# 384 unused bytes ahead of the x tiles: the moving operands shifted to the weights' address modulo 512

## The chip, the cores and the metric

The kernel runs on one core of a Trainium2 chip. The metric is device time in microseconds (us) of one execution. The runs before took 1220.17, 1220.52 and 1220.63 us; the median is 1220.52 us.

## What is computed

The reference is a causal convolution over seven steps with softmax weights per head, then a gated layer (SwiGLU, 192 to 1536 and back), then an ELU layer (192 to 2048 and back), all in float32:

```python
w = softmax(weight)                                   # (8 heads, 7 taps)
x = einsum('hk,bskhg->bshg', w, windows(x, 7))        # x: (2, 4096, 192) -> 8192 tokens of 192
g = x @ w_gate                                        # (192, 1536)
x = (g / (1 + exp(-g)) * (x @ w_val)) @ w_out         # (1536, 192)
h = x @ w_in                                          # (192, 2048)
out = where(h > 0, h, exp(min(h, 0)) - 1) @ w_out2    # (2048, 192)
```

## The kernel before

Tokens go through in 16 blocks of 512 (`TB`). Each block has a first layer (12 units j of 128 columns of both gate and value) and a second layer (16 units, taken two at a time). Stages of the two layers alternate over the blocks; the first two blocks are mixed while the weights still come in.

Every product is made in reduced-precision passes: an operand is split into a rounded part (`hi`) and the rest (`lo`), and hi·hi, lo·hi and hi·lo are summed in PSUM. The weights come as 64-bit words and are split once, into `in1hi`, `in1lo`, `in2hi`, `in2lo` (lines 386 and 387) and `out1`, `out2` (line 437), which stay in SBUF to the end. The activations are split block by block: x (the convolved input) and y (between the layers) into tiles of the pool `xp` (line 503), h (a layer's inner activations) into tiles of the pool `hp` (line 712).

On TensorE each matmul takes 64 rows (one half of the partitions, `lower` or `upper`), a stationary weight slice of 64x128 and a moving slice of 64x512. Two matmuls, one for each half of the rows, are always issued one after the other (lines 414 to 420 for the way into a layer, lines 467 and 468 for the way out), and the array runs both halves side by side. In this text a *step* is such a pair: one matmul of the lower half and one of the upper. Into a layer a unit takes nine steps, out of it five. For each matmul a weight load (LDWEIGHTS) of 128 columns goes ahead.

The order on all engines is written by a planner (class `Plan`) from fixed costs; it knows nothing of addresses. Tiles get their SBUF addresses from pools, which are laid one behind the other in the order in which they are made (lines 180 to 191). So a tile's address follows from the sizes of what was made before it.

One place in this kernel already has activations among the weights. While block 1's first layer runs, the second layer's weight tiles are still empty, and the h of its units j = 0 to 8 are written into them: even j into `in2hi` and `in2lo`, odd j into `out2` (lines 919 to 931, used by `split`, line 708). In the trace the matmuls that stream these read `c<-in2hi,out`, `c<-in2lo,out` and `c<-out,out`, where all others of the way out read `c<-h,out`. The first name after the arrow is the moving operand, the second the weights; buffer numbers are left out, so `out` stands for `out1` and `out2`.

Of the kernel before, what the change touches and what calls it, by code (L numbers as in the profile page):

```python
# [7 lines left out]
F32 = mybir.dt.float32  # L8
# [8 lines left out]
P = 128  # L17
# [147 lines left out]
def tile_conv_swiglu_elu(ctx: ExitStack, tc: tile.TileContext, x, weight, words, out, FF1, FF2):  # L165
# [16 lines left out]
    xs_p = ctx.enter_context(tc.tile_pool(name="xs", bufs=2))  # L182
    cv_p = ctx.enter_context(tc.tile_pool(name="cv", bufs=2))
    x_p = ctx.enter_context(tc.tile_pool(name="xp", bufs=1))
    y_p = ctx.enter_context(tc.tile_pool(name="yp", bufs=1))
    h_p = ctx.enter_context(tc.tile_pool(name="hp", bufs=7))
    t_p = ctx.enter_context(tc.tile_pool(name="tp", bufs=4))
# [882 lines left out]
```

## Time and profile before

| what | value |
|---|---|
| runs, median (lowest to highest) | 1220.52 us (1220.17 to 1220.63) |
| profiled execution, span from first to last instruction | 1218.3 us |
| median less span (what lies around the instructions) | 2.2 us |
| TensorE matmul (PE) busy | 1208.2 us, 99% |
| VectorE (DVE) busy | 990.4 us, 81% |
| ScalarE (ACT) busy | 837.2 us, 69% |
| DMA | 31.86 MB moved, mean 26 GB/s |

The page gives the profiled execution by its span alone. PE busy is the union of the matmuls' records; a matmul of 64x512 is recorded at about 391 ns although one starts about every 117 ns, so the records overlap and a busy PE says nothing of its pace. The pace is read from start to start.

### The profile page before, as it was taken

The numbers are of one execution on the slowest core, as the hardware profiler recorded it, in microseconds if no ns is written. First come the engines' busy times: TensorE is split into PE (matmuls) and PEld (weight loads), VectorE is DVE, ScalarE is ACT, GpSimd is POOL, SyncE is SP. The second block draws the span as 40 slices with busy tenths as digits, with TensorE's granted clock in tenths as the row PEclk, the third lists the DMA queues.
The fourth block names the chain that finished last, engine by engine and source line by source line (L and its number), as shares of the span: only waits on it lengthen the run. The fifth ranks groups of instructions, "written<-read, shape, count | busy, mean of one in ns | idle before, by whom it ended". The sixth has DMA issues, their size and how long they took to land.

```text
span 1218.3 us, 25292 instructions
## 1 busy us (share of the span) xinstructions
PE 1208.2 (99%) x10285; PEld 1143.1 (94%) x10285; DVE 990.4 (81%) x1632; ACT 837.2 (69%) x1556; POOL 2.1 (0%) x15
## 2 busy tenths in 40 slices
PE   8999999999999999999999999999999999999998
PEld 6899998999989999999999999999999999999987
DVE  8999999798695977959779596895968868495697
ACT  8878787585774857758477584866748667485686
POOL 0000000000000000000000000000000000000000
PEclk9999999999999999999999999999999999999999
DMA  5424000101000010000100001010000000000000
GB/s 187 143 64 142 14 19 6 49 1 36 1 23 15 1 36 1 23 14 1 36 1 23 14 3 34 1 34 4 10 14 1 23 1 11 13 1 15 2 14 14
DMA packets 18597, 31.86 MB, mean 26 GB/s; under 512 B 2864, under 2 KB 9008, under 8 KB 18480
## 3 DMA queue, kind: packets, MB, share of 16 engines
q1 hardware_dynamic: 18464, 30.25, 8.4%
q8 instruction: 80, 1.31, 0.5%
q14 instruction: 37, 0.30, 0.1%
q10 hardware_dynamic: 16, 0.00, 0.0%
HBM read 19.75 MB, written 6.29 MB: 21 GB/s over the span
## 4 chain that ended last, share of the span: by engine, by line
PE 98%; DVE 1%; ACT 0%; DMA 0%; issue 0%; DVEq 0%
PE c L468 43%; PE ph L416 22%; PE pv L416 18%; PE pg L416 15%; DVE cv L639 0%; DMA x<-x 0%; DMA wraw<-in_weight_dram 0%; ACT L222 0%; DVE w L323 0%; ACT words L338 0%; ACT x L538 0%; DVE p L845 0%; DVE o L890 0%; ACT o L886 0%; ACT cv L636 0%
## 5 line engine op out<-in xcount | busy, mean ns | idle before, releaser
L468 PE MATMUL c<-h,out 64*128 64x512 f32 x4390 | 707.9, 391 | 0.0
L468 PEld LDWEIGHTS c<-h,out 64*128 64x128 f32 x4390 | 554.3, 184 | 29.9
L416 PE MATMUL pv<-x,in1hi 64*128 64x512 f32 x1152 | 417.8, 393 | 0.0
L416 PE MATMUL pg<-x,in1hi 64*128 64x512 f32 x1152 | 411.1, 393 | 1.8 <-DMA x<-x 1.8
L716 ACT CAST h<-t 128x512 fp32r<-128x512 f32 x439 | 274.2, 625 | 176.3 <-DVE t L747 113.0
L720 DVE TENSOR_TENSOR h<-t,h 128x512 fp32r<-128x512 f32 x439 | 301.2, 687 | 80.5 <-ACT h L716 75.2
L416 PE MATMUL ph<-y,in2hi 64*128 64x512 f32 x1536 | 350.2, 392 | 0.0
L416 PEld LDWEIGHTS ph<-y,in2hi 64*128 64x128 f32 x1536 | 239.1, 184 | 8.0 <-DVE t L789 0.4
L416 PE MATMUL pg<-x,in1lo 64*128 64x512 f32 x576 | 225.6, 392 | 0.0
L416 PE MATMUL pv<-x,in1lo 64*128 64x512 f32 x576 | 225.6, 392 | 0.0
L416 PE MATMUL ph<-y,in2lo 64*128 64x512 f32 x768 | 222.1, 392 | 0.0
L416 PEld LDWEIGHTS pv<-x,in1hi 64*128 64x128 f32 x1152 | 212.2, 185 | 7.0 <-ACT x L538 0.3
L416 PEld LDWEIGHTS pg<-x,in1hi 64*128 64x128 f32 x1152 | 210.0, 185 | 9.1 <-ACT w L315 2.2
L747 DVE TENSOR_TENSOR t<-t,pv 128x512 f32<-128x512 f32 x192 | 131.4, 684 | 103.5 <-ACT t L743 79.8
L743 ACT ACTIVATE t<-pg 128x512 f32<-128x512 f32 x192 | 114.3, 595 | 139.6 <-PE pg L416 137.7
L785 DVE SCALAR_TENSOR_TENSOR t<-t,th 128x512 f32<-128x512 f32 x256 | 174.7, 686 | 25.5 <-ACT t L781 23.8
L789 DVE SCALAR_TENSOR_TENSOR t<-ph,t 128x512 f32<-128x512 f32 x256 | 172.6, 686 | 4.3
L777 ACT ACTIVATE th<-ph 128x512 f32<-128x512 f32 x256 | 153.2, 598 | 20.0 <-PE ph L416 18.2
L781 ACT ACTIVATE t<-ph 128x512 f32<-128x512 f32 x256 | 154.1, 602 | 0.0
L416 PEld LDWEIGHTS ph<-y,in2lo 64*128 64x128 f32 x768 | 129.4, 184 | 3.8
L639 DVE SCALAR_TENSOR_TENSOR cv<-xs,taps,cv 128x512 f32<-128x512 f32 (+1 forms) x180 | 109.6, 621 | 1.6
L416 PEld LDWEIGHTS pv<-x,in1lo 64*128 64x128 f32 x576 | 106.4, 185 | 3.0 <-DVE in1lo L350 0.2
(71 smaller groups left out, 566.8 us busy)
## 6 DMA issues: line engine op xcount, KB each, us to landing
words<-in_words_dram SPq DMA_DIRECT2D x34, 384.0 KB, 3.3
x<-x SPq DMA_DIRECT2D x64, 64.0 KB, 1.9
out_dram<-o SPq DMA_DIRECT2D x16, 256.0 KB, 2.0
xs<-in_x_dram SPq DMA_DIRECT2D x14, 259.0 KB, 3.0
out_dram<-o SPq DMA_DIRECT2D x16, 128.0 KB, 2.3
xs<-in_x_dram SPq DMA_DIRECT2D x30, 65.5 KB, 2.7
xs<-in_x_dram SPq DMA_DIRECT2D x2, 256.0 KB, 3.1
xs<-in_x_dram SPq DMA_DIRECT2D x2, 64.0 KB, 3.5
```

What stands on the lines that cost most here:

```text
L416: nc.tensor.matmul(p[bank][:, :n], w[r, k, g], m[r, s, :n], start=i == 0, stop=i == len(seq) - 1)
L468: nc.tensor.matmul(p[:, :n], lhs[r], m[r, :n], start=start, stop=stop)
L639: nc.vector.scalar_tensor_tensor(out=acc, in0=s, scalar=w, in1=acc, op0=ALU.mult, op1=ALU.add)
L716: nc.scalar.copy(parts[u][0][:, :n], live[u][0]["t"][:, :n])
L720: nc.vector.tensor_tensor(out=parts[u][1][:, :n], in0=live[u][0]["t"][:, :n], in1=raw(parts[u][0][:, :n]), op=ALU.subtract)
L743: nc.scalar.activation(out=box["t"][:, :n], in_=box["p"][0][:, :n], func=AF.Silu)
L747: nc.vector.tensor_tensor(out=t, in0=t, in1=box["p"][1][:, :n], op=ALU.mult)
L777: nc.scalar.activation(out=own["th"][:, :n], in_=box["p"][a][:, :n], func=AF.Tanh, scale=0.5)
L781: nc.scalar.activation(out=own["t"][:, :n], in_=box["p"][a][:, :n], func=AF.Exp)
L785: nc.vector.scalar_tensor_tensor(out=t, in0=t, scalar=1.0, in1=th, op0=ALU.add, op1=ALU.mult)
L789: nc.vector.scalar_tensor_tensor(out=t, in0=box["p"][a][:, :n], scalar=0.0, in1=t, op0=ALU.max, op1=ALU.min)
```

## The change

One line is added behind the making of the pool of the x tiles. The tile is never read or written.

```diff
     x_p = ctx.enter_context(tc.tile_pool(name="xp", bufs=1))
+    x_p.tile([P, 96], F32, tag="even", name="even")
     y_p = ctx.enter_context(tc.tile_pool(name="yp", bufs=1))
```

It takes 96 x 4 = 384 bytes of each partition, and all that is laid behind it moves up by 384 bytes. The instructions of all five engines, their order and their waits are the same in both programs. The byte addresses within a partition are:

| tiles | before | modulo 512 | after | modulo 512 |
|---|---|---|---|---|
| in1hi, in1lo, in2hi, in2lo, out1, out2 | 22368 to 126815 | 352 | the same | 352 |
| xs, cv (convolution) | 126816 to 137183 | 352, 416, 480 | the same | the same |
| x and y, hi and lo | from 137184 | 480 | from 137568 | 352 |
| h, hi and lo | from 163808 | 480 | from 164192 | 352 |
| t, th, words, w, o and the other tiles behind them | from 192480 | 480 and others | from 192864 | 352 and others |

A weight slice of 128 columns is 512 bytes and a moving slice 2048, so every slice of a tile has its tile's place modulo 512. The h of block 1 that lie in weight tiles have the place 352 in both programs.

## Rows read from the trace of the kernel before

**Rows 1.** The page: busy time by engine, and the granted clock over 40 slices
```profile
PE 1208.2 (99%) x10285; PEld 1143.1 (94%) x10285; DVE 990.4 (81%) x1632; ACT 837.2 (69%) x1556; POOL 2.1 (0%) x15
...
PEclk9999999999999999999999999999999999999999
```

**Rows 2.** The page: the chain that ended last, by engine
```profile
PE 98%; DVE 1%; ACT 0%; DMA 0%; issue 0%; DVEq 0%
```

**Rows 3.** TensorE's waits: total us, times, longest; the longest of four
```profile
PE pg L416 <- DMA x<-x: 1.8, 1, 1.8
```

**Rows 4.** Engines by stretch: stretch, its us, then busy us and instructions by engine
```profile
0.00:61.00 61.00, 56.36 (x411) 44.72 (x413) 55.48 (x110) 50.94 (x110) 1.95 (x13) 0.97 0.54 165
61.00:152.00 91.00, 91.00 (x787) 86.73 (x785) 89.31 (x167) 73.13 (x150) 0.00 (x0) 1.00 0.23 74
...
305.00:610.00 305.00, 305.00 (x2619) 292.08 (x2616) 239.02 (x384) 200.80 (x364) 0.00 (x0) 1.00 0.06 15
```

**Rows 5.** TensorE's matmuls by line and operands: count, busy us, mean ns of one
```profile
L468 PE MATMUL c<-h,out 64*128 64x512 f32 x4390 | 707.9, 391 | 0.0
...
L416 PE MATMUL pv<-x,in1lo 64*128 64x512 f32 x576 | 225.6, 392 | 0.0
L416 PE MATMUL ph<-y,in2lo 64*128 64x512 f32 x768 | 222.1, 392 | 0.0
...
L468 PE MATMUL c<-out,out 64*128 64x512 f32 x40 | 5.4, 388 | 0.0
L468 PE MATMUL c<-in2hi,out 64*128 64x512 f32 x30 | 5.0, 391 | 0.0
...
L468 PE MATMUL c<-in2lo,out 64*128 64x512 f32 x20 | 3.7, 391 | 0.0
```

**Rows 6.** TensorE's timeline, 87 to 99 us: start us, us, line, operands, count
```profile
87.82 0.64 PE L468 MATMUL c<-in2lo,out 64*128 64x512 f32 x4
88.30 1.31 PE L468 MATMUL c<-out,out 64*128 64x512 f32 x10
89.44 0.39 PE L416 MATMUL pg<-x,in1hi 64*128 64x512 f32 x1
89.45 0.39 PE L416 MATMUL pv<-x,in1hi 64*128 64x512 f32 x1
...
90.13 0.86 PE L468 MATMUL c<-in2hi,out 64*128 64x512 f32 x6
...
92.21 0.66 PE L468 MATMUL c<-in2lo,out 64*128 64x512 f32 x4
92.66 1.35 PE L468 MATMUL c<-out,out 64*128 64x512 f32 x10
93.80 0.39 PE L416 MATMUL pg<-x,in1hi 64*128 64x512 f32 x1
93.86 0.39 PE L416 MATMUL pv<-x,in1hi 64*128 64x512 f32 x1
...
98.16 0.39 PE L416 MATMUL pg<-x,in1hi 64*128 64x512 f32 x1
98.26 0.39 PE L416 MATMUL pv<-x,in1hi 64*128 64x512 f32 x1
```

**Rows 7.** TensorE's timeline, 1001 to 1010 us
```profile
1000.88 0.54 PE L416 MATMUL ph<-y,in2hi 64*128 64x512 f32 x2
...
1009.71 0.57 PE L416 MATMUL ph<-y,in2hi 64*128 64x512 f32 x2
```

**Rows 8.** TensorE's timeline, 481 to 499 us
```profile
482.65 0.54 PE L416 MATMUL ph<-y,in2hi 64*128 64x512 f32 x2
...
498.51 0.54 PE L416 MATMUL ph<-y,in2hi 64*128 64x512 f32 x2
```

**Rows 9.** The chain in order of time, 481 to 500 us: start us, us, what
```profile
481.32 1.64 PE c L468 x14
...
499.05 1.64 PE c L468 x14
```

## The prediction made before the run

> **What bounds the kernel.** I read the page first, then TensorE's waits, then the engines by stretch, then TensorE's groups, and last the timeline, start by start.
>
> The page gives TensorE 99% busy against 81% for VectorE, at the full granted clock (2.4 GHz) in every slice [rows 1], and the chain that ended last is 98% TensorE [rows 2]. Its longest wait of the whole execution is 1.8 us [rows 3]. So from the first stage on the time is the number of steps times the time of one step; nothing else can move it by per cents. What the reader is to see next is what one step takes. In the chain at 481 us two equal rows stand 17.73 us apart (499.05 less 481.32) [rows 9], with 152 matmuls, or 76 steps, between them: 233.3 ns a step. The stretch of 305 us counts 2619 matmuls, some three of which straddle its edges, so 1308 steps and 233.2 ns [rows 4]. The group rows show that a matmul does not take the same for all operands: `c<-out,out`, with h of block 1 in the weight tile, records 388 ns where `c<-h,out` and the x and y groups record 391 and 392 [rows 5].
>
> **The two halves have paces of their own.** At 1001 us the pair row grows from 0.54 to 0.57 us over 38 steps [rows 7]: the leading half takes 8.83 us, or 232.4 ns a step, the other 8.86, or 233.2 ns. At 482 us the pair row is 0.54 at both ends of 15.86 us [rows 8], so there the halves run in step, and the pace is 233.3 ns, the slower one's. I read this as: a half may slide ahead within a bounded lead, then waits for the other. The slower half sets the time.
>
> **The change, part by part.** It adds no instruction, wait or byte moved; the instruction orders are the same. Its only parts are addresses.
>
> (1) xs, cv and the weights stay. Cost nothing.
>
> (2) t, th, words, w and the output tiles move with the rest. They are read and written by VectorE, ScalarE and DMAs, which after 152 us have slack: VectorE is busy 239.0 of 305 us [rows 4]. I take nothing for them. If VectorE gained or lost one per cent, that would be worth at most 0.9 us, in the stretch from 61 to 152 us, where it is busy 89.3 of 91 us [rows 4].
>
> (3) x, y and h move from place 480 to place 352, the weights' place. No row streams x, y or an ordinary h from there, but the 90 matmuls on the held h do [rows 5], and they bound it. From 89.44 to 98.16 us two rounds of 38 matmuls each pass, of which 20 in each stream from place 352 (ten `c<-out`, six `c<-in2hi`, four `c<-in2lo`) and 18 from x at place 480 [rows 6]. The leading half does its 38 steps in 98.16 less 89.44, 8.72 us, 229.5 ns each. The other does them in 98.26 less 89.45, 8.81 us, 231.8 ns. Both are faster than at 1001 us, with a little over half of the operands moved. Taking the effect as proportional to the share, the slower half goes from 233.3 to 233.3 less 1.5 x 38/20, some 230.4 ns; that is 2.85 ns saved a step. The faster goes from 232.4 by 2.9 x 38/20 to some 226.9 ns. A check within one run of `c<-out`: from 88.30 to 89.44 and from 92.66 to 93.80 five steps take 1.14 us, 228 ns [rows 6].
>
> The sum: from 152 us to the end of the span, 1066 us, there are 1066/0.2333 = 4570 steps. At the slower half's saving that is 4570 x 2.85 ns = 13.0 us. Before 152 us I take nothing: there 390 steps would save 1.1 us, but VectorE at 98% is next [rows 4], and it would make TensorE wait for the weights' splitting. Span 1218.3 less 13.0 is 1205.3 us; with the 2.2 us that lie between the span and the median, 1207.5 us. The rows have 10 ns, so 8.81 us may be off by 10 ns, 0.5 ns a step after scaling, 2.3 us in the end.
>
> The bounds. From above: if both halves went as the faster one does, 233.3 to 226.9 ns, the gain is 4570 x 6.4 ns = 29 us. From below: the held rows also have steps that are slow. From 87.82 to 88.30 two steps on `c<-in2lo` take 0.48 us, 240 ns each [rows 6], after x at the other place. If steps like these became a third of all, the others staying, the loss is 4570/3 x 6.7 ns = 10.2 us. I take the value between, nearest to the row with the most steps behind it, the slower half's 8.81 us.
>
> One rule speaks against any gain. The Trainium skill, "SBUF — State Buffer", section "Who interferes with whom", has TensorE read its moving operand and its weights through two independent ports and wait for nobody; by it the place of a tile cannot matter, and the time would stay at 1220.5 us. The 388 against 391 ns is a mark against that rule, from 40 matmuls in one place of the run. It is the third case below.
>
> **The rivals.**
>
> (a) The slower half sets the pace at 230.4 ns: 1207.5 us, my forecast, with 1202 to 1214 us as its own range. For it: halves in step at the slower pace [rows 8], and the slower half faster in the mixed stretch [rows 6].
>
> (b) Both halves settle at the fast pace, 226.9 ns: 1220.5 less 29 is 1191 us. For it: within a run of ten on `c<-out` the leading half holds 228 ns without a break. Against it: the other half's rows in the same stretch, 231.8 ns.
>
> (c) The place does nothing, and the held rows are fast for another reason: they come at the time of the weight loads, ten in a row, and the `c<-in2hi` and `c<-in2lo` groups, at the same place, record 391 ns like all others [rows 5]. Also, held h lie 864 bytes into their kilobyte and the moved tiles will lie 352 bytes in; if more than 512 bytes count, the held rows are no model. Then the halves keep 233.3 ns: 1220.5 us. Against it: the two rounds around 90 us are faster as wholes, x included.
>
> (d) Slower. With all at one place, the weight slice that is loaded for the next matmul of a half and the slice that streams meet at the same place whenever their timing is alike, and a step takes the 240 ns of the `c<-in2lo` pair at 87.82 us [rows 6]. With one step in three so and no gain elsewhere, 1220.5 plus 10.2 is 1230.7 us. It decides against the gain of (a) from the share f at which 6.7 f = 2.85 (1 - f), some 30% of the steps. Against it: the 388 ns mean of `c<-out`, where stream and weights are already at one place.
>
> **How the numbers follow.** Chances: (a) 0.55, (b) 0.13, (c) 0.18, (d) 0.14. The time is that of (a), 1207.5 us. The three runs before lie within 0.46 us, so 0.2%, 2.4 us, is about what can be told from no change. (a) and (b) are faster, and a little of (c) that still gains more than 2.4 us: 0.69. Within 0.2%: 0.17. Slower: 0.14. The range takes in (a) and (c) whole and the near part of (b), and leaves out the far part of (b) and most of (d): 1193 to 1222 us.
>
> **What would show it.** If (a): `c<-h,out` records some 388 to 389 ns in place of 391, the x and y groups with it; two rows 152 matmuls apart in the chain at 481 us stand 17.5 us apart in place of 17.73; the stretch from 305 to 610 us counts some 2650 matmuls; pair rows grow or shrink faster than 0.8 ns a step until the halves lock. If (b), 386 ns or less and 17.25 us. If (c), 391 and 17.73. If (d), group means over 394 ns. The stretch before 152 us should end at most 1 us earlier than now. I would be wrong at the root if the time moved without the step moving: by a new wait of TensorE, of which the waits list, with 1.8 us at the top now, would have a row of several us; or if the gain lay in the first 152 us.

## The result and the profile after

The changed kernel takes 1199.57 us (median of four runs, 1198.64 to 1199.98) against 1220.35 us for the kernel before beside it. The ratio is 0.9834, with a 95% interval of 0.9819 to 0.9849: it is faster by 20.8 us. The forecast was 1207.5 us with a range of 1193 to 1222. Over all sets of runs the kernel before took some 1216 us in 13 of its 55 executions and some 1220 us in the others, which no kept trace explains, so that a ratio of runs is not quite the ratio of the medians; one execution of another kernel, which took 3082 us, counts in no ratio.

The page of the changed kernel, busy time by engine and the chain by engine, reads:

```profile
PE 1184.6 (99%) x10285; PEld 1135.6 (95%) x10285; DVE 989.0 (83%) x1632; ACT 831.8 (69%) x1556; POOL 2.1 (0%) x15
...
PE 77%; DVE 13%; ACT 7%; issue 2%; DMA 0%; SPq 0%; DVEq 0%; ACTq 0%
```

VectorE and ScalarE are busy for nearly the same time as before [rows 1]; TensorE has 23.6 us less. The chain, 98% TensorE before [rows 2], now runs for a fifth of the span through VectorE and ScalarE. That is the first sign that the gain was larger on TensorE than in the end.

TensorE's groups in the changed kernel (count, busy us, mean ns of one, idle time before and its releasers) answer to [rows 5]:

```profile
L469 PE MATMUL c<-h,out 64*128 64x512 f32 x4390 | 691.6, 387 | 3.6 <-DVE p L846 3.1 <-DVE h L721 0.4
...
L417 PE MATMUL ph<-y,in2hi 64*128 64x512 f32 x1536 | 345.4, 387 | 0.4 <-DVE t L790 0.4
...
L417 PE MATMUL pv<-x,in1lo 64*128 64x512 f32 x576 | 222.7, 387 | 0.1
L417 PE MATMUL ph<-y,in2lo 64*128 64x512 f32 x768 | 220.1, 387 | 0.0
...
L469 PE MATMUL c<-in2hi,out 64*128 64x512 f32 x30 | 6.4, 394 | 0.1
L469 PE MATMUL c<-out,out 64*128 64x512 f32 x40 | 6.0, 386 | 0.0
```

The large groups have come down from 391 to 393 ns to 387 or 388. Of the three small groups on held h, which lay at the weights' place before too, `c<-out` went from 388 to 386, but `c<-in2hi` rose from 391 to 394 and `c<-in2lo` from 391 to 392; in the replanned kernel below all three record 386. The chain in order of time shows the step, at the place of [rows 9]:

```profile
470.24 1.59 PE c L469 x14
...
478.87 1.59 PE c L469 x14
...
487.49 1.59 PE c L469 x14
```

From 478.87 to 487.49 us 38 steps pass in 8.62 us, 226.8 ns each, where 76 steps took 17.73 us before. The halves keep their distance while they do, as the timeline shows (the answer to [rows 7] and [rows 8]): the pair rows stay at 0.58 us.

```profile
481.47 0.58 PE L417 MATMUL ph<-y,in2hi 64*128 64x512 f32 x2
...
485.78 0.58 PE L417 MATMUL ph<-y,in2hi 64*128 64x512 f32 x2
```

So in this stretch both halves run at the pace to which the prediction had scaled the faster half's of the mixed rounds. Over the whole stretch of 305 us it looks different; this row answers to the third of [rows 4]:

```profile
305.00:610.00 305.00, 303.76 (x2664) 292.31 (x2662) 241.45 (x388) 203.88 (x373) 0.00 (x0) 1.00 0.05 15
```

2664 less three is 1330 steps in 305 us, 229.3 ns each in the mean. The difference of 2.5 ns a step is waiting. Weight loads and matmuls have new entries among the waits (total us, times, longest):

```profile
PEld c L469 <- DVE p L846: 6.6, 10, 0.7
PEld c L469 <- DVE o L846: 3.6, 12, 0.3
...
PE c L469 <- DVE p L846: 3.1, 10, 0.3
```

Before, the longest wait of TensorE's matmuls was 1.8 us [rows 3] and that of its weight loads 2.2 us, and no add of a layer's sums (L845 there, L846 here) was among its releasers. The timeline around one such place:

```profile
503.74 0.69 DVE L721 TENSOR_TENSOR h<-t,h 128x512 fp32r<-128x512 f32 x1
...
504.35 0.68 DVE L846 TENSOR_TENSOR p<-p,c 128x512 f32<-128x512 f32 x1
504.36 0.40 PE L469 MATMUL c<-h,out 64*128 64x512 f32 x1
...
505.08 1.10 PE L469 MATMUL c<-h,out 64*128 64x512 f32 x5 [0.32 <-DVE p L846]
```

From 504.36 to 505.08 us TensorE does one step in the time of three: it needs the sums' PSUM banks, which the add frees, and the add stands on VectorE behind a split of h (L721).

### The profile page after: what moved, and what is told of

It is laid out like the page before. It is cut to its first block, busy times and chain, and to the rows that moved or that the text cites. A ratio compares the mean times of both kernels' runs of the same rounds, so it can differ in the third digit from the quotient of the medians.

```text
span 1196.9 us, 25292 instructions
## 1 busy us (share of the span) xinstructions
PE 1184.6 (99%) x10285; PEld 1135.6 (95%) x10285; DVE 989.0 (83%) x1632; ACT 831.8 (69%) x1556; POOL 2.1 (0%) x15
## 4 chain that ended last, share of the span: by engine, by line
PE 77%; DVE 13%; ACT 7%; issue 2%; DMA 0%; SPq 0%; DVEq 0%; ACTq 0%
PE c L469 34%; PE ph L417 21%; PE pv L417 14%; PE pg L417 8%; DVE h L721 2%; ACT h L717 2%; DVE cv L640 2%; DVE t L790 2%; DVE t L748 2%; ACT L223 1%; DVE t L786 1%; ACT t L744 1%; DVE x L542 1%; DVE p L846 1%; DVE w L343 1%
## 5 line engine op out<-in xcount | busy, mean ns | idle before, releaser
L469 PE MATMUL c<-h,out 64*128 64x512 f32 x4390 | 691.6, 387 | 3.6 <-DVE p L846 3.1
L469 PEld LDWEIGHTS c<-h,out 64*128 64x128 f32 x4390 | 561.0, 184 | 23.8 <-DVE p L846 6.6
L417 PE MATMUL pv<-x,in1hi 64*128 64x512 f32 x1152 | 400.8, 387 | 0.0
L721 DVE TENSOR_TENSOR h<-t,h 128x512 fp32r<-128x512 f32 x439 | 301.5, 687 | 80.5 <-ACT h L717 75.2
L417 PE MATMUL ph<-y,in2hi 64*128 64x512 f32 x1536 | 345.4, 387 | 0.4 <-DVE t L790 0.4
L417 PEld LDWEIGHTS ph<-y,in2hi 64*128 64x128 f32 x1536 | 259.1, 184 | 6.8 <-DVE t L790 1.5
L417 PE MATMUL pg<-x,in1lo 64*128 64x512 f32 x576 | 222.8, 387 | 0.0
L417 PE MATMUL pv<-x,in1lo 64*128 64x512 f32 x576 | 222.7, 387 | 0.1
L417 PEld LDWEIGHTS pv<-x,in1hi 64*128 64x128 f32 x1152 | 207.3, 184 | 5.8 <-ACT words L339 0.3
L417 PEld LDWEIGHTS ph<-y,in2lo 64*128 64x128 f32 x768 | 139.0, 184 | 1.9
```

The source lines that it names most:

```text
L417: nc.tensor.matmul(p[bank][:, :n], w[r, k, g], m[r, s, :n], start=i == 0, stop=i == len(seq) - 1)
L469: nc.tensor.matmul(p[:, :n], lhs[r], m[r, :n], start=start, stop=stop)
L721: nc.vector.tensor_tensor(out=parts[u][1][:, :n], in0=live[u][0]["t"][:, :n], in1=raw(parts[u][0][:, :n]), op=ALU.subtract)
```

## The experiments

T1 to T4 are theories on the addresses, W on the waits, V on the plan alone, M on which of the weights hold a stream up. The ratios are against the kernel before on the same chip.

**Both at place 480.** The weights are moved too, so that they and x, y, h lie together at another place. Compared with the next kernel, x, y, h and all behind them have the same addresses; only the weights (and xs and cv) differ.

```diff
     wts = ctx.enter_context(tc.tile_pool(name="wts", bufs=1))
+    wts.tile([P, 32], F32, tag="evenw", name="evenw")
 ...
     x_p = ctx.enter_context(tc.tile_pool(name="xp", bufs=1))
+    x_p.tile([P, 96], F32, tag="even", name="even")
```

> 128 unused bytes ahead of the weights and 384 ahead of x: weights, x, y and h all lie at place 480 modulo 512. Theory T1, the moving operand and the weights have to lie at the same place: fast, a step of 226.7 ns, 1197 to 1202 us. Theory T2, the place of the moving operand alone decides (480 is bad, 352 good, wherever the weights are): 233 ns a step, 1218 to 1223 us. Theory T3, other tiles (t, words, outputs) or address bits above 512 matter: no certain value, but the same as e2_pad_512, which has all of x, y, h and the tiles behind them at the very same addresses as this kernel.

Measured: 1199.44 us, ratio 0.9829 (0.9813 to 0.9846).

**512 bytes in place of 384.**

```diff
+    x_p.tile([P, 128], F32, tag="even", name="even")
```

> The unused tile has 512 bytes in place of 384: x, y, h and all behind them move, but keep place 480 modulo 512, with the weights at 352. T1 and T2: nothing changes against the kernel before, 1218 to 1223 us, 233 ns a step. T3, bits above 512 or just the moving away of the tiles counts: faster, near 1200 us.

Measured: 1220.09 us, ratio 0.9995 (0.9983 to 1.0007). The two groups, first with both at 480, then with 512 bytes:

```profile
L470 PE MATMUL c<-h,out 64*128 64x512 f32 x4390 | 696.0, 387 | 3.5 <-DVE p L847 3.0 <-DVE h L722 0.4
```

```profile
L469 PE MATMUL c<-h,out 64*128 64x512 f32 x4390 | 726.6, 392 | 0.0
```

The same x, y and h, at the same addresses, stream at 387 ns with the weights at 480 and at 392 ns with the weights at 352. T2 and T3 fall: it is the place of one against the other.

**x and y alone, h alone.** In the first, 384 bytes ahead of x and 128 ahead of h, so that h is back at 480; in the second, 384 bytes ahead of h alone. `gap_p` is a pool of its own.

```diff
     x_p = ctx.enter_context(tc.tile_pool(name="xp", bufs=1))
+    x_p.tile([P, 96], F32, tag="even", name="even")    # not in the second
 ...
+    gap_p = ctx.enter_context(tc.tile_pool(name="gap", bufs=1))
+    gap_p.tile([P, 32], F32, tag="gap", name="gap")    # 96 in the second
     h_p = ctx.enter_context(tc.tile_pool(name="hp", bufs=7))
```

> x and y at place 352 as in the changed kernel, h and all behind it at place 480 as before. T1 with shares: x and y are moving operand in 57% of the matmuls, so 0.57 of the way of the step from 233.3 to 226.7 ns, some 229.5 ns and 1205 to 1212 us. Rival T4, the halves keep in step only where every stream is at the weights' place, and a mixed program has no gain: 1217 to 1222 us.

Measured: 1212.22 us, ratio 0.9934 (0.9919 to 0.9949).

> h and all behind it at place 352, x and y at place 480 as before. T1 with shares: h streams in 43% of the matmuls, so 0.43 of the way, some 230.5 ns a step and 1208 to 1215 us. T4: 1217 to 1222 us. If the tiles behind h (t, words, outputs) made the gain: 1200 us.

Measured: 1208.28 us, ratio 0.9903 (0.9888 to 0.9917). From 305 to 610 us, x and y alone and then h alone:

```profile
305.00:610.00 305.00, 305.00 (x2639) 301.43 (x2637) 240.40 (x386) 200.59 (x365) 0.00 (x0) 1.00 0.05 15
```

```profile
305.00:610.00 305.00, 305.00 (x2646) 290.17 (x2644) 240.29 (x387) 201.21 (x366) 0.00 (x0) 1.00 0.06 15
```

No wait of a matmul is over 2.0 us in either; with three matmuls straddling, the steps are 231.4 and 230.8 ns. T4 falls, since both gain. But T1's shares are not right either: x and y, 57% of the matmuls, brought 1.9 ns a step where 3.8 were expected, and 1212.22 us lie just above the range of 1205 to 1212; h with 43% brought 2.5 ns where 2.8 were expected, and its time is inside its range. Together that is 4.4 ns a step, where moving both brings 6.5. Two groups of each kernel, x and y alone first, show that the gain does not go stream by stream:

```profile
L471 PE MATMUL c<-h,out 64*128 64x512 f32 x4390 | 757.2, 390 | 0.4 <-DVE h L723 0.4
...
L419 PE MATMUL pg<-x,in1lo 64*128 64x512 f32 x576 | 224.3, 389 | 0.0
```

```profile
L470 PE MATMUL c<-h,out 64*128 64x512 f32 x4390 | 694.6, 389 | 0.0
...
L418 PE MATMUL pg<-x,in1lo 64*128 64x512 f32 x576 | 223.9, 389 | 0.0
```

In each kernel one of the two streams lies at the weights' place and the other does not, and both record 389 or 390 ns, neither 387 nor 392. So a stream at the weights' place has less than its full gain when streams at another place stand beside it, and those have some of the gain too. How they act on each other is not shown.

**Other distances.** 128, 256, 416 and 448 bytes in the same line put x, y and h at 96, 224, 384 and 416, with the weights at 352.

> The unused tile has 128 bytes: x, y and h lie at place 96 modulo 512, the weights at 352, which is 256 apart. T1a, places count modulo 512 and only coincidence is fast: no gain, 1212 to 1225 us. T1b, places count modulo 256 (or less): 96 and 352 coincide, a step of 226.7 ns and 1197 to 1202 us. T1c, the distance counts by degrees, and the kernel before (128 apart) is not the worst: slower than before, 1222 to 1235 us.

Measured: 1199.47 us, ratio 0.985 (0.9828 to 0.9872), `c<-h,out` at 387 ns.

> The unused tile has 256 bytes: x, y and h lie at place 224, 128 below the weights at 352 (before they lay 128 above). If the distance counts alike on both sides: 1218 to 1223 us as before. If the direction counts (the weights are read behind the stream that ends at the moving operand's place): a different step, anything from 227 to 240 ns, 1200 to 1240 us. A fast step of 226.7 ns here would end T1a.

Measured: 1220.07 us, ratio 1.0002 (0.9986 to 1.0019), `c<-h,out` at 392 ns.

> The unused tile has 416 bytes: x, y and h lie at place 384, 32 bytes past the weights at 352. T1a, only coincidence is fast: 1212 to 1225 us. T1c, by degrees: 32 bytes cost a quarter of what 128 bytes cost, a step of some 228.3 ns, 1201 to 1207 us.

Measured: 1220.89 us, ratio 1.0018 (1.0005 to 1.0031).

> The kernel with x, y, h at place 384, 32 bytes past the weights, once more for its trace, since the first execution with a profile took 3082 us, all others 1221. All or nothing: c<-h records 391 to 392 ns as at 128 bytes, 1221 us. If its time comes from new waits of TensorE and not from the step: c<-h at 388 ns and a waits list of over 10 us.

Measured: 1221.29 us in a single run, `c<-h,out` at 392 ns; the waits list holds 1.6 us at most, so it is the step.

> x, y and h at place 416, 64 bytes past the weights at 352. All or nothing, modulo 256: 1218 to 1223 us, c<-h at 391 to 392 ns. A period of 64 bytes, or distances that count by degrees: faster, 1200 to 1215 us.

Measured: 1219.6 us, ratio 0.9992 (0.9982 to 1.0002), `c<-h,out` at 392 ns.

Distances of 0 and 256 bytes are fast; 32 and 64 bytes past the weights and 128 on either side are slow, and all as slow as each other within 1.7 us of the medians. Places count modulo 256, not 512, and at the distances tried either they coincide or they don't: T1b is right on the period, T1a on all or nothing, and T1c (by degrees) falls.

**Which weights hold a stream up.** The changed kernel with in1lo alone at place 480.

```diff
             self.hi = wts.tile([P, n, 3, P], F32R, name=f"{name}hi")
+            if name == "in1":
+                wts.tile([P, 32], F32, name="ahead")
             self.lo = wts.tile([P, n, 3, P], F32R, name=f"{name}lo")
+            if name == "in1":
+                wts.tile([P, 96], F32, name="behind")
```

> The changed kernel with in1lo alone at place 480, all other weights and x, y, h at 352. Within one half of the rows in1lo is loaded while the matmul before it, on in1hi, streams. M1, a stream is held up by the weight load that goes on beside it: the in1lo groups record 386 to 388 ns, and the in1hi groups rise by some 3 ns in the mean, since half of them have a load of in1lo beside them. M2, a stream is held up by the place of its own weights: the in1lo groups rise to 391 to 395 ns, the in1hi groups stay at 387 to 388. In both the second layer (ph) stays at 387, and the time rises by 576 steps x up to 6.7 ns, at most 3.9 us: 1199 to 1204 us. M3, a stray place upsets all streams of the layer: over 1206 us.

Measured: 1203.99 us, ratio 0.9868 (0.9851 to 0.9884). The groups:

```profile
L421 PE MATMUL pg<-x,in1hi 64*128 64x512 f32 x1152 | 417.2, 392 | 2.0 <-DMA x<-x 2.0
L421 PE MATMUL pv<-x,in1hi 64*128 64x512 f32 x1152 | 406.9, 391 | 0.0
L421 PE MATMUL ph<-y,in2hi 64*128 64x512 f32 x1536 | 341.8, 387 | 0.3 <-DVE t L794 0.3
L421 PE MATMUL pv<-x,in1lo 64*128 64x512 f32 x576 | 226.8, 394 | 0.0
```

Both rose: in1hi by some 4 ns in the mean, as M1 says for half of them, and in1lo by 6 to 7 ns, as M2 says. The second layer stays at 387 ns, so M3 falls. The time is inside both ranges' 1199 to 1204 us, at their upper end. Which matmuls of in1hi are slow can be read from start to start, here along the leading half of one unit:

```profile
500.14 0.39 PE L421 MATMUL pg<-x,in1hi 64*128 64x512 f32 x1
...
500.37 0.39 PE L421 MATMUL pg<-x,in1lo 64*128 64x512 f32 x1
...
500.61 0.39 PE L421 MATMUL pg<-x,in1hi 64*128 64x512 f32 x1
...
500.83 0.39 PE L421 MATMUL pg<-x,in1hi 64*128 64x512 f32 x1
...
501.06 0.39 PE L421 MATMUL pg<-x,in1lo 64*128 64x512 f32 x1
...
501.30 0.39 PE L421 MATMUL pg<-x,in1hi 64*128 64x512 f32 x1
...
501.52 0.79 PE L473 MATMUL c<-h,out 64*128 64x512 f32 x4
```

From in1hi to in1lo it takes 0.23 us, from in1lo to in1hi 0.24, and from in1hi to in1hi or to h 0.22. The starts in the trace from 150 to 1180 us give 232.5 ns for a matmul on in1hi that in1lo follows (914 of them), 227.5 ns where in1hi follows (386), and 233.9 ns for one on in1lo that in1hi follows (924). So a step was long when its own weights lay elsewhere, as M2 says, and also when the weights loaded beside it did, as M1 says; each is half of the answer. What in the chip holds them up stays open.

**The plan for the faster step.** The changed kernel, and the kernel before, with one number of the planner changed.

```diff
-        return plan.add("pe", 0.233, 0.64, emit, needs, new, uses)
+        return plan.add("pe", 0.227, 0.64, emit, needs, new, uses)
```

> The changed kernel, with the planner told that a step of TensorE takes 0.227 us in place of 0.233; TensorE's order stays, the orders of ScalarE and VectorE are planned anew. Theory W1: some 8 us of the step's gain went into waits of TensorE for the last adds of a layer (L846), because ScalarE's and VectorE's orders were planned for a slower TensorE; then the waits shrink and the time is 1190 to 1197 us. Rival W2: the waits come from the chain of ScalarE and VectorE work itself, which no order shortens: 1197 to 1202 us, waits on L846 as in the changed kernel. Rival W3: the table of numbers that sets the order is fitted to the old plan, and the new one is worse: over 1202 us.

Measured: 1190.63 us (1190.52 to 1190.71), ratio 0.9778 (0.9757 to 0.98), the fastest of all. Its chain by engine, and its row from 305 to 610 us:

```profile
PE 97%; DVE 1%; DMA 1%; ACT 0%; SPq 0%; issue 0%
```

```profile
305.00:610.00 305.00, 305.00 (x2686) 276.49 (x2685) 244.05 (x393) 209.22 (x378) 0.00 (x0) 1.00 0.05 15
```

TensorE is the bound again, with 1341.5 steps, 227.4 ns each; the waits for L846 have left the lists of its matmuls and weight loads. W1 holds, and W2 and W3 fall.

> The kernel before, addresses unchanged, with the planner told that a step takes 0.227 us. V1: the new plan is worth something only where TensorE really steps in 226.7 ns; here TensorE is the bound at 233.3 ns with no waits to remove: 1217 to 1222 us. V2: the new plan is better by itself, by the 9 us that it gave the changed kernel: 1210 to 1214 us. V3: the plan is wrong for the slow step and makes waits: over 1223 us.

Measured: 1220.29 us, ratio 1.0006 (0.9997 to 1.0015). V1: without the place, the plan is worth nothing. So the place alone brought 20.8 us, and with a plan that fits 29.4 us (1220.06, the kernel before in the same set of runs, less 1190.63).

## Why the prediction was right, and where its size was off

**The bound and the part that counts.** Right for the kernel before: the time is steps times the time of a step, and only part (3), x, y and h, mattered. Part (2) at nothing: the kernel with both at 480 has t, words and the outputs at the very addresses of the 512-byte kernel, still at their place of before, and is as fast as the changed one.

**The natural experiment.** The h held in weight tiles showed the direction before any run, and the reason given there, one place for stream and weights, is shown by the two kernels that differ in the place of the weights (and of xs and cv, which the change leaves where they were). The doubt in rival (c), that more than 512 bytes might count, was a wrong fear: fewer count, 256.

**The term that was mis-sized.** The saving of the slower half, 2.85 ns a step and 13.0 us, was scaled from rounds in which 20 of 38 matmuls streamed from the weights' place, by 38/20. The saving is 6.5 ns (233.3 to 226.8), and the 226.9 ns that rival (b) had for both halves is what the chain after shows, down to the 17.25 us for 76 steps (487.49 less 470.24). What failed is the proportion: the kernels with x and y alone or h alone show 1.9 and 2.5 ns a step in mixed stretches, 4.4 ns together, where all at one place bring 6.5, so a share of 20 in 38 shows less than its share of the gain. That the slower half must set the pace was no objection, since with all at one place neither is slower.

**What was left out.** Rival (b) came to 1191 us and was not reached either: some 9 us of it became waits, most of them for the adds at a layer's end. The prediction looked for the next limit in the first 152 us, where VectorE was 98% busy, and not in the order of VectorE's and ScalarE's work, which was written for a step of 233 ns; 79% busy said that there is time, not that it comes at the right moment. The replanned kernel shows this cost: 8.9 us (1199.57 less 1190.63; 8.8 us against the 128-byte kernel in the same set of runs). Two errors of opposite sign left the forecast 7.9 us too high. That the time fell inside the range is in part luck: without the waits it would have been near 1191 us, below the 1193 us of the range's lower end.

**The signs named ahead.** `c<-h,out` was to fall to 388 or 389 ns and fell to 387; the count from 305 to 610 us was to be 2650 and is 2664. Pair rows were to grow or shrink until the halves lock; in the stretch shown they stay at 0.58 us. Waits of several us were named as a sign of error at the root; they came, as a cost beside the gain. Before 152 us the changed kernel is 13 matmuls ahead, 1211 against 1198 [rows 4]:

```profile
0.00:61.00 61.00, 58.02 (x417) 49.73 (x419) 55.40 (x110) 50.71 (x110) 1.95 (x13) 1.00 0.53 165
61.00:152.00 91.00, 90.81 (x794) 86.21 (x792) 89.83 (x169) 73.47 (x152) 0.00 (x0) 1.00 0.23 74
```

That is some 1.5 us, more than the 1 us that was set as the most; but the granted clock in the first 61 us was 1.00 here and 0.97 before, so not all of it need come from the step.

The Trainium skill's "SBUF — State Buffer", section "Who interferes with whom", by which TensorE reads weights and moving operand through independent ports and waits for nobody, does not agree with these runs: 392 against 387 ns for the same streams, with only the weights (and tiles of the convolution) moved. Whether it is the two reads that wait for each other is not shown.

## What to carry to other kernels

Where TensorE is the bound with a fresh weight load for each matmul, compare the addresses of weights and moving operands; in this kernel the same place modulo 256 bytes was worth 6.5 ns a step, 2.8% of it, for 128 unused bytes a partition. Look for places in the trace where some operands happen to lie elsewhere, but don't scale a mixed stretch in proportion. When the bounding engine becomes faster, plan the others anew for its new pace: that was 8.9 us more here, and nothing without the faster step.

## What the runs showed of the hardware that was not expected

- The recorded time of a matmul depends on the distance between its stream and the weights modulo 256 bytes, all or nothing: 387 ns at 0 and 256, 392 ns at 32, 64 and 128.
- The mean hides two kinds of step. In the kernel before, from 150 to 1180 us, the starts of one half lie 229 or 230 ns apart in 40% of the steps and 237 or 238 ns in 32%; in the changed kernel 95% are 226 or 227 ns.
- In the slow case one half of the rows can run at 232.4 and the other at 233.2 ns a step [rows 7]; in the fast case both run at 226.8 ns at a constant distance.
